# Attention and soft MoE on one core: another layout of the row-sum transfers, the norm's scaling and mask in one instruction, a new order, and eight combinations of the left half in a row

## The chip, the core and the metric

The kernel runs on one core of a Trainium2 chip. The metric is device time in microseconds (us) of one execution. TensorE (PE in the rows) does the matrix products and transposes, VectorE (DVE) and ScalarE (ACT) read and write PSUM and SBUF, GpSimd (POOL) works on SBUF, and SyncE (SP) issues nearly all transfers. Each engine runs its own instructions in the order written for it and waits on semaphores for the others.

## What is computed

Eight batches of eight heads, 576 positions, width 64. Each head has causal softmax attention and a memory read, mixed by a gate; the result goes through a soft mixture of eight experts.

```python
scores = scale * q @ k.T ; causal mask ; a = softmax(scores)          # per head
local = a @ v
q_p = phi(q)                                                          # elu + 1
mem_out = (q_p @ M_prev) / (q_p . z_prev + 1e-6)
x = g * mem_out + (1 - g) * local                                     # -> (4608, 512)
logits = x @ phi
d = softmax over all 4608 rows ; slot_input = d.T @ x                 # 8 experts x 4 slots
slot_out = relu(slot_input @ w1) @ w2
out = softmax over slots(logits) @ slot_out
```

All data is float32 (the scores are made from a high and a low part of q and k, three products each).

## The kernel before

**Pairs.** Two heads are handled together: 32 pairs, written `@0` to `@31`. `SEQ` is a list of some 2480 step names in the order in which they are issued; `name@n:slots` calls `op_name(n)` and says which PSUM bank it takes. `EV` says for movable steps whether ScalarE (`a`), GpSimd (`p`) or VectorE (`v`) does them. So `SEQ` and `EV` fix the order on every engine, the SP queue among them.

**One pair.** `loadq`, `loadk`, `loadv`, `loadm` fetch inputs. `qhi`, `qlo`, `kn`, `kl` make the high and low parts in the single buffers `X` and `K2`; they can be written only after the last score product of the pair before. `s4`, `s3`, `s2`, `s1`, `sa` (line 399, 418) are the score products of the four 128-row blocks and of the first 64 rows; `max` (line 469) masks and takes the row maximum, `exp` (line 478) the exponent and the row sum. `t`, `tf`, `ta` transpose the probabilities on TensorE (lines 565, 571, 575), `te`, `tfe`, `tae` bring them to SBUF, `av`, `ava` and `u4` (lines 603 to 629) multiply by v and the memory. `mo`, `xm`, `xa` (lines 643 to 655) scale and add into `xt`.

**The row sums' way.** Nine sums per row block stand in a 128 x 9 tile. `rec` inverts them times the gate, `rt` transposes them on TensorE to 9 x 128, `rte` copies them to `rts`, `rrw` writes them to DRAM (`rs`), and `rrr` reads them back, spread over 64 partitions for each head, into `rm` (576 wide). `mo` and `xa` need `rm`.

**The norm's way.** `norm` (line 522) makes q_p . z in PSUM; `neps` adds 1e-6 and multiplies by the gate, `nmk` multiplies by a mask, `nred` sums and inverts, `nrw` writes 4.5 KB to DRAM (`rd`), `nrr` reads it back spread into `rb`, and `qn` (line 554) multiplies q_p by it; `u4` needs `qn`.

**Weights.** `w@0` to `w@46` are loads of 512 KB each of the experts' weights, put among the steps: 29 go to buffers of their own (`w@0` to `w@28`), the others into buffers of the attention as these come free (`WORD`). All go through the SP queue, as do the small transfers above.

**Behind the pairs.** The `x` and `y` steps do the dispatch softmax and slot inputs. Then `f1` (line 949) and `f2` (line 966) are the experts' two layers, for the output's left half (`dh` 0) and right half (`dh` 1); `piece(k)` issues k parts of the right half's second layer. `comb(dh, t4)` (line 1011) makes a 512-row block of the output half, copies it by ScalarE and VectorE, and writes 512 KB out. `g1` and `g2` (lines 997, 1001) scale and sum the expert outputs ahead of the combinations. `fl` steps are matmuls without use, to keep TensorE going while it waits.

## Time and profile before

| | |
|---|---|
| median of 3 runs | 455.71 us (452.76, 455.71, 455.92) |
| profiled execution's own time | 454.65 us |
| its span, first to last instruction | 452.9 us |
| around the span | 1.75 us |
| busy: TensorE, VectorE, ScalarE, GpSimd | 424.7, 344.2, 332.8, 153.5 us |
| transferred | 97.42 MB |

A row of the timeline gives start and length of a merged group of like instructions, and in square brackets the time that the engine had been idle ahead of it and what ended that. TensorE's matmuls are pipelined, so lengths overlap. Transfers of the SP queue have issue times only; when they landed shows in whoever waited for them.

### The profile page before, as it was taken

The page shows a single profiled execution, that of the slowest core. Times are in us where ns is not written, and L with a number is a line of the kernel's source. Part 1 is how long each engine was busy: PE and PEld are TensorE (multiplying, and loading weights), DVE is VectorE, ACT ScalarE, POOL GpSimd, SP SyncE. Part 2 cuts the span into 40 slices and gives each one's busy share as a digit, 9 for nine tenths or more (in the row PEclk, how much of TensorE's full clock was granted, in tenths as well). Part 3 has the DMA queues.
Part 4 walks back from the last instruction along what each step waited for, and adds up shares of the span by engine and source line. Part 5 has one row for each costly group of instructions (what it writes and reads, how often), then busy time and mean ns, then how long its engine had stood idle before and what let it go on. Part 6 is the DMA issues. An engine that isn't in the chain of part 4 may idle for free.

```text
span 452.9 us, 12441 instructions
## 1 busy us (share of the span) xinstructions
PE 424.7 (94%) x4364; PEld 281.2 (62%) x4364; DVE 344.2 (76%) x1200; ACT 332.8 (73%) x947; POOL 153.5 (34%) x165
## 2 busy tenths in 40 slices
PE   8997999999899999999899999999999988999981
PEld 4764766666666766776566665766666655635540
DVE  5886889989799898889786996998989852431541
ACT  4997888979796988889778896989789861221431
POOL 2453443434344443353342364336343510000000
PEclk9999999999999999999999999999999999999997
DMA  4587647677856757765867558547664399999888
GB/s 157 151 253 205 190 111 241 199 204 224 236 175 199 217 152 201 221 207 153 284 194 225 162 153 237 143 143 203 178 175 127 86 335 316 334 375 397 271 289 283
DMA packets 65710, 97.42 MB, mean 215 GB/s; under 512 B 14704, under 2 KB 41072, under 8 KB 65648
## 3 DMA queue, kind: packets, MB, share of 16 engines
...
q14 instruction: 27, 0.22, 0.1%
q10 hardware_dynamic: 288, 0.09, 0.1%
...
## 4 chain that ended last, share of the span: by engine, by line
PE 64%; DVE 13%; DMA 11%; issue 4%; ACT 3%; SPq 2%; POOL 1%; DVEq 0%; POOLq 0%; ACTq 0%
PE psS L399 11%; PE psT L603 11%; PE psT L565 10%; DMA rm<-rs 6%; PE psT L624 5%; DVE P L469 4%; PE pf L966 3%; PE pf L949 3%; PE psT L727 3%; PE psT L571 2%; PE pp L1011 2%; DMA m<-in_M_dram 2%; PE psT L522 2%; DVE xt L643 2%; DMA rb<-rd 2%
## 5 line engine op out<-in xcount | busy, mean ns | idle before, releaser
L478 ACT ACTIVATE P<-P,nm 128x320 f32<-128x320 f32 (+4 forms) x288 | 166.1, 587 | 7.7 <-DVE nm L469 7.1
L469 DVE CUSTOM_DVE_ANT_0 P<-psS,mq 128x192 f32<-128x192 f32 (+3 forms) x256 | 133.6, 548 | 9.9 <-PE psS L399 8.8
L333 ACT COPY at<-psT 128x512 f32<-128x512 f32 (+1 forms) x187 | 94.3, 553 | 29.9 <-PE psT L565 11.4
L399 PE MATMUL psS<-K,X 64*128 64x288 f32 (+3 forms) x960 | 88.2, 319 | 3.6 <-DVE nm L469 3.4
L565 PE MATMUL psT<-cs,P 128*128 128x128 f32 x640 | 87.1, 276 | 4.4 <-DVE xt L654 2.4
L399 PEld LDWEIGHTS psS<-K,X 64*128 64x128 f32 x960 | 69.3, 185 | 25.9 <-issue 9.1
L603 PE MATMUL psT<-at,mq 128*64 128x256 f32 (+3 forms) x512 | 83.5, 443 | 0.0
L565 PEld LDWEIGHTS psT<-cs,P 128*128 128x128 f32 x640 | 70.8, 142 | 10.8 <-issue 4.2
L478 ACT ACTIVATION_READ_ACCUMULATOR P<-P,nm 128x1 f32 x288 | 57.2, 199 | 0.0
L385 POOL TENSOR_TENSOR X<-mq,X 128x512 fp32r<-128x512 f32 x31 | 40.8, 1315 | 24.0 <-DVE X L336 10.7
L391 POOL TENSOR_TENSOR K<-kq,K 128x576 fp32r<-128x576 f32 x27 | 38.5, 1428 | 10.0 <-DVE nm L469 5.3
L603 PEld LDWEIGHTS psT<-at,mq 128*64 128x64 f32 x512 | 28.8, 136 | 17.8 <-issue 9.3
L624 PE MATMUL psT<-kq,m 64*64 64x512 f32 x64 | 34.2, 614 | 1.3 <-DVE kq L554 1.3
L625 PE MATMUL psT<-at,mq 64*64 64x512 f32 x64 | 34.2, 615 | 0.0
L627 PE MATMUL psT<-kq,m 64*64 64x512 f32 x64 | 34.2, 615 | 0.0
L626 PE MATMUL psT<-at,mq 64*64 64x512 f32 x64 | 34.2, 614 | 0.0
L643 DVE TENSOR_TENSOR xt<-psT,rm 128x448 f32<-128x448 f32 (+7 forms) x60 | 23.8, 435 | 13.6 <-DMA rm<-rs 5.3
L338 POOL TENSOR_SCALAR X<-mq 128x512 fp32r<-128x512 f32 x21 | 13.0, 619 | 53.2 <-PE psT L489 20.9
L509 POOL TENSOR_SCALAR kq<-mq 128x576 f32<-128x576 f32 x22 | 15.4, 700 | 39.2 <-PE psT L629 39.0
L338 POOL TENSOR_SCALAR K<-kq 128x576 fp32r<-128x576 f32 x17 | 11.8, 691 | 49.3 <-PE psS L399 35.8
L516 DVE SCALAR_TENSOR_TENSOR kq<-mq,kq 128x576 f32<-128x576 f32 x32 | 26.1, 814 | 2.2 <-ACT mq L512 2.0
L336 DVE COPY at<-psT 128x512 f32<-128x512 f32 (+2 forms) x45 | 25.0, 563 | 3.2 <-PE psT L565 1.8
(198 smaller groups left out, 686.9 us busy)
## 6 DMA issues: line engine op xcount, KB each, us to landing
...
```

What stands on the lines that cost most here:

```text
L333: nc.scalar.copy(o, i)
L385: ALU_ENG[ev("qlo", n)].tensor_tensor(out=X[:, 1, :], in0=st[n]["q"][:, 64:576], in1=X[:, 0, :].bitcast(F32), op=ALU.subtract)
L391: ALU_ENG[ev("kl", n)].tensor_tensor(out=K2[:, 1, :], in0=st[n]["k"][:, 0:S], in1=K2[:, 0, :].bitcast(F32), op=ALU.subtract)
L399: nc.tensor.matmul(out(h), X[ROW[h], x, 128 * i - 128:128 * i], K2[ROW[h], y, o + k0:o + k1], start=(x, y) == (0, 0), stop=(x, y) == (0, 1))
L469: nc.vector.tensor_tensor_reduce(out=sm, in0=src, in1=msk, op0=ALU.add, op1=ALU.min, scale=-0.125, scalar=3.0e38, accum_out=s["nm"][:, J:J ...
L478: nc.scalar.activation(sm, sm, AF.Exp, scale=-1.0, bias=s["nm"][:, J:J + 1], accum_out=s["sum"][:, J:J + 1])
L565: nc.tensor.transpose(out=ps[:, 256 * x + 128 * h:256 * x + 128 * h + 128], in_=chunk(n, i, h, c), identity=ident)
L603: nc.tensor.matmul(s["oa"][ROW[h], 512 - w:512], vt[:, c, ROW[h]], at[:, base + 512 * h:base + 512 * h + w], start=first, stop=s["parts"] ...
L624: nc.tensor.matmul(om[ROW[0], :], s["m"][ROW[0], 0:64], s["qp"][ROW[0], 64:576], start=True, stop=True)
L625: nc.tensor.matmul(w2(s["oa"][ROW[1], :]), vt[ROW[0], 4, ROW[1]], af[ROW[0]], start=first, stop=s["parts"] == 5)
L626: nc.tensor.matmul(w2(s["oa"][ROW[0], :]), vt[ROW[1], 4, ROW[0]], af[ROW[1]], start=first, stop=s["parts"] == 5)
L627: nc.tensor.matmul(om[ROW[1], :], s["m"][ROW[1], 0:64], s["qp"][ROW[1], 64:576], start=True, stop=True)
```

## The change

Five edits.

**Sums' transfers.** The nine sums are put in another order (four blocks of head 0, the first rows of both, four blocks of head 1), so that `rrw` is one transfer of 9 x 128 instead of three, and `rrr` three instead of two: 64 x 512 and 64 x 64 for head 0, 64 x 576 for head 1.

**Norm.** `neps` and `nmk` become one VectorE instruction with a table `mg` made once by `gate` (mask times gate). Before, `neps` was on ScalarE in 12 pairs and on VectorE in 20, `nmk` on GpSimd in 24 and on VectorE in 8.

**A new order.** `SEQ` and `WORD` are new throughout, and `EV`: on GpSimd stand 21 `kn` (17 before), 25 `qhi` (21), 29 `kl` (27), 30 `qlo` (31), 24 `qrelu` (22); on ScalarE 10 `kn` (15), 4 `qhi` (6), 144 `te` (139), 5 `x5e` (none); on VectorE 16 `te` (21), 3 `kl` (5), 3 `qhi` (5), 8 `qrelu` (10), 2 `x5e` (7). All four conversions of a pair are on GpSimd in 18 pairs (14 before).

**Fillers.** 13 filler matmuls become 8: the four of `fl.4@0`, ahead of the second pair's scores, give way to two more groups of transposes of the first pair, and `fl.5.s` at the last pair's wait is a `fl.2.s`.

**Combinations.** Eight combinations of the left half are issued in a row, and the ninth behind `g1(1)`.

```diff
-loadq@1 qhi@0 kn@0 loadm@0 qlo@0 loadk@1 qrelu@0 kl@0 gate@0 s4@0:01 max.40@0 qexp@0 max.41@0 exp.40@0 qphi@0 fl.2@0:0
+loadk@1 qhi@0 kn@0 qrelu@0 loadq@1 qlo@0 loadm@0 kl@0 qexp@0 loadv@0 gate@0 s4@0:01 qphi@0 max.41@0 max.40@0 exp.41@0 fl.2@0:0
...
     def op_gate(n):
         nc.vector.tensor_scalar(out=rm[:, 976:1056], in0=rm[:, 976:1056], scalar1=1.0, scalar2=None, op0=ALU.add)
-        nc.vector.tensor_scalar(out=epg, in0=gc[:, :, 9], scalar1=1e-6, scalar2=None, op0=ALU.mult)
+        nc.vector.tensor_tensor(out=mg, in0=maskn.rearrange("a (o u) -> a o u", o=1).broadcast_to([128, NP, 16]),
+                                in1=gc[:, :, 9:10].broadcast_to([128, NP, 16]), op=ALU.mult)
...
     def op_rrw(n):
         rts = st[n]["rts"]
-        rd = st[n]["rs"] = drm.tile([2, S], F32, name="rs")
-        for h in range(2):
-            nc.sync.dma_start(out=rd[h, 64:S].rearrange("(i x) -> i x", i=4), in_=rts[4 * h:4 * h + 4])
-        nc.sync.dma_start(out=rd[:, 0:64].rearrange("h (j x) -> j h x", j=1), in_=rts[8:9].rearrange("j (h x) -> j h x", h=2))
+        rd = st[n]["rs"] = drm.tile([9, 128], F32, name="rs")
+        nc.sync.dma_start(out=rd, in_=rts)
 
     def op_rrr(n):
-        for h in range(2):
-            nc.sync.dma_start(out=rr[ROW[h]], in_=st[n]["rs"][h].rearrange("(o x) -> o x", o=1).broadcast_to([64, S]))
+        rd = st[n]["rs"]
+        z = rd[0:1]
+        for o, w, x, h in ((64, 512, 0, 0), (0, 576, 576, 1), (0, 64, 512, 0)):
+            nc.sync.dma_start(out=rr[ROW[h], o:o + w], in_=bass.AP(tensor=z.tensor, offset=z.offset + x, ap=[[0, 64], [1, w]]))
...
     def op_neps(n):
         rn = st[n]["rn"] = sml.tile([128, 144], F32, name="rn", bufs=1)
-        if ev("neps", n) == "a":
-            nc.scalar.activation(rn, st[n]["nps"][:, 0:144], AF.Identity, bias=epg[:, n % NP:n % NP + 1], scale=gc[:, n % NP, 9:10])
-        else:
-            nc.vector.tensor_scalar(out=rn, in0=st[n]["nps"][:, 0:144], scalar1=1e-6, scalar2=gc[:, n % NP, 9:10], op0=ALU.add, op1=ALU.mult)
-
-
-    def op_nmk(n):
-        rn = st[n]["rn"].rearrange("a (u x) -> a u x", x=9)
-        ALU_ENG[ev("nmk", n)].tensor_tensor(out=rn, in0=rn, in1=maskn.rearrange("a (u o) -> a u o", o=1).broadcast_to([128, 16, 9]), op=ALU.mult)
+        nc.vector.scalar_tensor_tensor(out=rn.rearrange("a (u x) -> a u x", x=9), in0=st[n]["nps"][:, 0:144].rearrange("a (u x) -> a u x", x=9), scalar=1e-6,
+                                       in1=mg[:, n % NP].rearrange("a (u o) -> a u o", o=1).broadcast_to([128, 16, 9]), op0=ALU.add, op1=ALU.mult)
...
     piece(1)
-    for t4 in range(NQ):
+    for t4 in range(NQ - 1):
         comb(0, t4)
     piece(13)
     g1(1)
+    comb(0, NQ - 1)
     g2(1)
     for t4 in range(NQ):
         comb(1, t4)
```

Three places where the order moves, as the instructions stand on an engine (numbers behind a name tell buffers apart).

**SP queue, pairs 0 and 1** (`rs<-rts` and `rm<-rs` are the sums' transfers, `rd<-rq` and `rb<-rd` the norm's, `w0` to `w2` the weights). Before:

```order
L504 DMA rm_105<-rs_323 64x576 x2
L544 DMA rd_394<-rq_379 128x9
L769 DMA w0_396<-in_w1_dram 128x1024
L376 DMA m_402<-in_M_dram 128x96
L371 DMA mq_102<-in_v_dram 128x640
L499 DMA rs_432<-rts_428 4x128 x2
L500 DMA rs_432<-rts_428 2x1x64
L550 DMA rb_455<-rd_394 64x4x144 x2
L769 DMA w1_474<-in_w1_dram 128x1024
L361 DMA mq_102<-in_q_dram 128x704
L366 DMA kq0_103<-in_k_dram 128x640
L504 DMA rm_105<-rs_432 64x576 x2
```

Now:

```order
L498 DMA rm_105<-rs_335 64x512
L498 DMA rm_105<-rs_335 64x576
L498 DMA rm_105<-rs_335 64x64
L355 DMA mq_102<-in_q_dram 128x704
L365 DMA mq_102<-in_v_dram 128x640
L370 DMA m_411<-in_M_dram 128x96
L492 DMA rs_421<-rts_409 9x128
L537 DMA rb_430<-rd_346 64x4x144 x2
L355 DMA mq_102<-in_q_dram 128x704
L498 DMA rm_105<-rs_421 64x512
L498 DMA rm_105<-rs_421 64x576
```

The two weight loads between the sums of pair 0 and those of pair 1 are gone from here; the first weight load now stands behind pair 3's sums, and one k load has moved behind pair 1's `rm`.

**SP queue, the last pair** (`rs_5987` before and `rs_5927` now are pair 31's sums, `rb_6010` and `rb_5936` its norm). Before:

```order
L544 DMA rd_5948<-rq_5935 128x9
L771 DMA K2_5951<-in_w2_dram 128x1024
L771 DMA P3_5956<-in_w2_dram 128x1024
L371 DMA mq_102<-in_v_dram 128x640
L499 DMA rs_5987<-rts_5978 4x128 x2
L500 DMA rs_5987<-rts_5978 2x1x64
L771 DMA mq_102<-in_w2_dram 128x1024
L550 DMA rb_6010<-rd_5948 64x4x144 x2
L771 DMA P3_6043<-in_w2_dram 128x1024
L504 DMA rm_105<-rs_5987 64x576 x2
```

Now:

```order
L531 DMA rd_5872<-rq_5862 128x9
L758 DMA P4_5878<-in_w2_dram 128x1024
L758 DMA P3_5889<-in_w2_dram 128x1024
L365 DMA mq_102<-in_v_dram 128x640
L492 DMA rs_5927<-rts_5920 9x128
L537 DMA rb_5936<-rd_5872 64x4x144 x2
L758 DMA kq0_5957<-in_w2_dram 128x1024
L498 DMA rm_105<-rs_5927 64x512
L498 DMA rm_105<-rs_5927 64x576
L498 DMA rm_105<-rs_5927 64x64
```

One weight load that stood ahead of `rb` now stands behind it, and one that stood ahead of `rm` stands behind that.

**TensorE, the last instructions** (line 1011, now 998, is `comb`; line 1001, now 988, `g2(1)`; `x36` counts matmuls). Before:

```order
L966 MATMUL pf<-w_6426,at 32x256
L966 MATMUL pf<-w_6428,at 32x256
L966 MATMUL pf<-w_6430,at 32x256
L966 MATMUL pf<-w_6432,at 32x256
L1001 MATMUL pp<-xk,cs 128x256
L1011 MATMUL pp<-xk,cT 128x256 x36
```

Now:

```order
L953 MATMUL pf<-w_6358,at 32x256
L953 MATMUL pf<-w_6360,at 32x256
L953 MATMUL pf<-w_6362,at 32x256
L953 MATMUL pf<-w_6364,at 32x256
L998 MATMUL pp<-xk,cT 128x256 x4
L988 MATMUL pp<-xk,cs 128x256
L998 MATMUL pp<-xk,cT 128x256 x36
```

The four matmuls of the left half's ninth combination stand between the last product of the second layer and `g2(1)`.

## Rows read from the trace of the kernel before

**Rows 1.** The page: busy time, share of the span and instructions, by engine.

```profile
PE 424.7 (94%) x4364; PEld 281.2 (62%) x4364; DVE 344.2 (76%) x1200; ACT 332.8 (73%) x947; POOL 153.5 (34%) x165
```

**Rows 2.** Busy time by stretch: length, each engine, clock, DMA share, GB/s.

```profile
50.00:100.00 50.00, 49.97 (x506) 35.10 (x502) 44.58 (x164) 43.06 (x122) 19.39 (x21) 1.00 0.67 197
365.00:380.00 15.00, 12.26 (x115) 7.79 (x113) 5.32 (x15) 6.46 (x20) 1.79 (x2) 1.00 1.04 327
```

**Rows 3.** Timeline of TensorE: rows with an idle time ahead of them.

```profile
14.10 1.06 PE L399 MATMUL psS<-K,X 64*128 64x288 f32 x12 [0.56 <-DVE nm L469]
...
38.95 0.71 PE L399 MATMUL psS<-K,X 64*128 64x320 f32 x6 [2.34 <-DVE nm L469]
...
110.11 0.63 PE L565 MATMUL psT<-cs,P 128*128 128x128 f32 x4 [0.15 <-DVE ext L336]
122.62 0.45 PE L522 MATMUL psT<-kq,m 128*32 128x144 f32 x8 [1.62 <-DMA m<-in_M_dram]
...
222.88 0.63 PE L565 MATMUL psT<-cs,P 128*128 128x128 f32 x4 [1.54 <-DVE xt L643]
...
358.58 0.28 PE L489 MATMUL psT<-cs,r 128*9 128x128 f32 x1 [0.35 <-DVE r L484]
...
380.50 0.61 PE L624 MATMUL psT<-kq,m 64*64 64x512 f32 x1 [1.16 <-DVE kq L554]
```

**Rows 4.** Timeline of VectorE: three waits for transfers.

```profile
38.14 0.23 DVE L654 TENSOR_TENSOR xt<-psT,rm 128x64 f32<-128x64 f32 x1 [3.27 <-DMA rm<-rs]
...
379.59 0.76 DVE L554 TENSOR_TENSOR kq<-kq,rb 128x576 f32<-128x576 f32 x1 [5.57 <-DMA rb<-rd]
382.28 0.22 DVE L654 TENSOR_TENSOR xt<-psT,rm 128x64 f32<-128x64 f32 x1 [1.93 <-DMA rm<-rs]
```

**Rows 5.** Timeline of the SP queue at the last pair: start and length of issues.

```profile
369.46 0.60 SPq L499 DMA_DIRECT2D rs<-rts  x2
370.11 0.61 SPq L500 DMA_DIRECT2D rs<-rts  x1
371.14 0.36 SPq L771 DMA_DIRECT2D mq<-in_w_dram  x1
371.61 1.39 SPq L550 DMA_DIRECT2D rb<-rd  x2
373.87 0.36 SPq L771 DMA_DIRECT2D P<-in_w_dram  x1
374.57 1.11 SPq L504 DMA_DIRECT2D rm<-rs  x2
```

**Rows 6.** Instructions by line and shape: count, busy us, mean ns, idle before.

```profile
L529 DVE TENSOR_SCALAR rn<-psT,rm 128x144 f32<-128x144 f32 x20 | 7.3, 363 | 2.4 <-PE psT L522 2.3
L527 ACT ACTIVATE rn<-psT,rm 128x144 f32<-128x144 f32 x12 | 5.7, 479 | 1.5 <-PE psT L522 1.4
L534 POOL TENSOR_TENSOR rn<-rn,rm 128x144 f32<-128x144 f32 x24 | 11.7, 489 | 33.5 <-ACT rn L527 24.8 <-DVE rn L529 8.5
L746 DVE SCALAR_TENSOR_TENSOR acc<-acc,al,psT 128x256 f32<-128x256 f32 x14 | 6.5, 467 | 0.6 <-PE psT L742 0.4 <-ACT at L333 0.2
```

**Rows 7.** The chain that ended last, in its last part: start, length, what.

```profile
427.29 5.79 PE pf L966 x104
...
433.10 0.49 DVE xk L997
...
433.64 0.71 PE pp L1001 x2
...
434.80 0.72 PE pp L1011 x8
```

**Rows 8.** Timeline of GpSimd: first and last of the four conversions of pair 15.

```profile
165.70 0.89 POOL L338 TENSOR_SCALAR K<-kq 128x576 fp32r<-128x576 f32 x1 [6.29 <-PE psS L399]
...
168.53 1.27 POOL L385 TENSOR_TENSOR X<-mq,X 128x512 fp32r<-128x512 f32 x1
```

**Rows 9.** Timeline of TensorE: the first score products of pair 15.

```profile
170.80 1.05 PE L399 MATMUL psS<-K,X 64*128 64x288 f32 x12
```

More of the change, by code (lines that the diff above doesn't have):

```diff
@@ new lines @@
+t.3@9:1 w@5 max.a@10 te.1@9 max.20@10 t.4b@9:2 w@6 tae@9 te.3@9 max.30@10 t.4a@9:3 exp.a@10 qhi@11 tf@9:0 max.21@10
+te.4a@9 max.31@10 norm@10:1 qlo@11 exp.11@10 rrr@9 av.0@9:3 max.10@10 exp.21@10 neps@10 te.4b@9 tfe@9 ava@9:1 qn@9
+loadq@12 s4@11:01 exp.20@10 nred@10 loadk@12 exp.40@10 nrw@10 av.3@9 max.41@11 av.2@9 w@7 exp.31@10 x2s@1 u4@9:0
+exp.10@10 exp.30@10 max.40@11 av.1@9 qrelu@11 loadm@11 exp.41@11 rec@10 s1@11:0 xa@9 loadv@10 exp.40@11 s3@11:1 x1d@1
+mo@9 qexp@11 s2@11 nrr@10 xm@9 t.1@10:2 kn@12 rt@10:1 max.11@11 t.3@10:3 rte@10 te.1@10 kl@12 x5@1:0 sa@11 rrw@10
@@ new lines @@
+max.10@27 te.3@26 qlo@28 rrw@26 max.30@27 t.2@26:2 tae@26 w@26 te.1@26 x5@5:0 max.31@27 tf@26:3 w@27 te.2@26 kn@28
+t.4b@26:1 max.20@27 loadq@29 exp.30@27 tfe@26 av.0@26:2 kl@28 te.4b@26 max.11@27 max.21@27 exp.20@27 rrr@26 norm@27:3
+x4.1@5:1 x5e@5 neps@27 qn@26 exp.40@27 s4@28:01 nred@27 exp.11@27 nrw@27 exp.10@27 av.3@26 max.40@28 av.1@26 loadk@29
+exp.31@27 x4a.1@5 ava@26:0 av.2@26 exp.a@27 max.41@28 exp.21@27 u4@26:3 rec@27 rt@27:1 qrelu@28 loadv@27 s1@28:0
+loadm@28 s3@28:1 qexp@28 max.11@28 mo@26 s2@28 rte@27 rrw@27 ta@27:1 xa@26 t.3@27:2 kn@29 tae@27 nrr@27 max.31@28
@@ new lines @@
+rte@30 loadm@31 qexp@31 rrw@30 s1@31:1 xa@29 exp.40@31 s2@31 nrr@30 mo@29 t.4b@30:1 max.30@31 t.4a@30:3 te.4b@30 w@29
+xm@29 t.1@30:0 te.4a@30 w@30 t.3@30:1 qphi@31 te.1@30 rrr@30 t.2@30:2 te.3@30 max.10@31 tf@30:3 max.20@31 te.2@30
+ta@30:0 norm@31:1 w@31 tae@30 exp.30@31 x4.1@6:2 neps@31 exp.10@31 nred@31 av.0@30:0 qn@30 exp.20@31 max.a@31 x4a.1@6
+nrw@31 tfe@30 x5@6:1 max.21@31 w@32 ava@30:2 exp.a@31 av.3@30 max.31@31 av.2@30 w@33 exp.21@31 max.11@31 u4@30:3
+exp.31@31 exp.11@31 av.1@30 x5e@6 rec@31 xa@30 rt@31:1 mo@30 loadv@31 t.3@31:2 rte@31 t.1@31:1 rrw@31 te.3@31 xm@30
@@ L198 @@
+yz@y y12@y y10.1@y fl.1@0:2 w@46 y12e@y y10e.1@y y10e.0@y
 """.split()
@@ L244 @@
[L244 to L247 removed]
+        qhi@0 qlo@0 kl@0 qlo@1 te.4a@0 rte@0 qn@0 qrelu@2 tae@1 te.4b@1 tfe@1 tae@2 te.4a@3 qn@3 rte@4 x2a@0
```

413 lines of the change are left out of this document (195 added, 218 removed).

## Prediction, made blind

> **What bounds the kernel now.** I read the page first. It shows TensorE busy for 424.7 of 452.9 us, so no engine but TensorE can be short of time over the whole [rows 1]. Then the busy times by stretch. In an ordinary stretch of the pairs, 50 to 100 us, TensorE is busy for 49.97 of 50 us, and VectorE and ScalarE for 44.6 and 43.1: less work on those two gives nothing there of itself [rows 2]. What a new order can win is the time that TensorE stands. So the third view was TensorE's timeline, with the idle time ahead of each row [rows 3]. There are four kinds of it.
>
> First, the fill: 0.56 us ahead of pair 1's scores and 2.34 us at 38.95 us [rows 3]. VectorE's timeline tells why the second: it stood 3.27 us for pair 1's sums (`rm`) [rows 4]. Second, between 50 and 365 us there are 12 idle times of 0.15 us or more, the first at 110.11 and the last at 358.58 us, 6.5 us in all; the two largest, 1.62 and 1.54 us, end with a late transfer, of M and (through VectorE's `mo`) of the sums [rows 3]. Third, the end of the pairs: the queue moves 327 GB/s at a full DMA share [rows 2], because weights are loaded into the freed buffers, and the last pair's two small transfers wait their turn: `rb` is issued at 371.61 and is used at 379.59 us, `rm` is issued at 374.57 and used at 382.28 [rows 4, 5]. TensorE runs fillers and still stands 1.16 us [rows 3]. Fourth, the turn between the output's halves: the last product of the second layer ends at 433.08 us, `g1` and `g2` follow, and the first combination of the right half starts at 434.80 [rows 7].
>
> **The norm's instruction.** Removed are 20 VectorE instructions of 363 ns, 12 of ScalarE of 479 ns, and the mask, of which 24 on GpSimd took 489 ns [rows 6]. Added are 32 on VectorE that no row shows. From below they cost 363 ns as the plain scaling of the same 144 columns, from above 467 ns as the same kind of instruction on 256 columns [rows 6]; I take 370, as the size decides. VectorE gets 12 more of them, some 4 us, and loses its 8 masks and several conversions; ScalarE loses 5.7 us, GpSimd 11.7 us [rows 6]. All of it lies beside TensorE's products, so the sum has nothing for it. If that cover were gone, VectorE's 12 x 0.37 = 4.4 us would be the price. The way from `norm` to `rd` gets shorter by about 0.5 us and one engine change, which only helps the last pair, and there `rb` waits behind the sums anyway.
>
> **The sums' transfers.** Three issues of 0.60 us together for two and 0.61 for the third [rows 5] become one. As the single one has the plain shape of one of the pair, I take 0.3 us; so the write starts 0.9 us earlier for its last part. `rrr` issues three times instead of two, at 1.11 us for two [rows 5] 0.55 us more, before the last part lands. The way from `rte` to `mo` is shorter by 0.35 (first rows of head 0) to 0.9 us. In most pairs it hides; it is worth something only where `rm` is late.
>
> **The fill.** In the changed order no weight load stands ahead of pair 1's sums (two did, each 512 KB; at the 327 GB/s of [rows 2] 1.6 us each, 3.2 us in all, about the 3.27 us that VectorE stood). The bounds are 0 and 2.34 us, what TensorE stood; I take 2.0. Ahead of pair 1's scores stand transposes of pair 0 in place of four fillers. Those are useful work moved into a time that was lost; bounds 0 and 1.5 (the idle 0.56 and as much again in fillers); I take 0.5, because ScalarE, which must copy the transposes out, is the next in line. The weight loads that left have to go somewhere: 29 of them now stand between pair 4 and pair 30.
>
> **The ordinary pairs.** By the listing of the order, more of TensorE's work stands between `rrr` and its use (in the median about 0.7 us more), and fewer bytes between `rte` and `rrr`. Three of the twelve idle times are of that kind, the largest of them 1.54 us [rows 3]. The two last answers of this order differ in sign: the window in which GpSimd refills `X` and `K2` gets shorter by some 0.4 us in the median pair. Bounds: 3 us gained (those three waits gone) and 3 us lost (as many new ones elsewhere); I take 1.0 gained.
>
> **The last pair.** `rb` was held at the queue by the sums' write and by one weight load: its issue came 2.15 us after the first write's [rows 5]. Now it follows one issue, so it is issued 1.7 us earlier. The queue is full, so what counts is also what lies ahead: 512 KB less for `rb` and for `rm` each, 1.6 us at 327 GB/s [rows 2]. Both bounds nearly agree. Since u4 waits for `rb` and `xa` for `rm`, both must come earlier, and both do: 1.6 us. The end of ScalarE's exponents of the last pair, which releases `rt` and so `rrw`, comes earlier by the norm's 0.48 us [rows 6], of which I take 0.2. That is 1.8 us; bounds 0.9 (the larger part eaten by something late upstream) and 3. Fewer fillers there cost nothing, as they stood in idle time.
>
> **The halves.** Of the 1.72 us from 433.08 to 434.80 us, the ninth combination fills a part: its matmuls (0.72 us for eight [rows 7]) run while `g1` (0.49 us) is on VectorE, and `g2` follows. The first row of combinations gets shorter by those 0.72 us and by what they waited there for copies (some 0.3, an estimate); `g2` waits for them 0.2 us longer than for `g1`: I take 0.8 us; bounds 0 and 1.2. The output's transfers are issued as blocks are ready, and the end of the span follows the first block of the right half, so this gain reaches the end. The left half's last block now goes out later, in a time in which the queue would stand.
>
> **Sum.** 2.0 + 0.5 + 1.0 + 1.8 + 0.8 = 6.1 us. The profiled execution took 454.65 us (span 452.9 and 1.75 around it): 448.5 us. The median of the three runs is 1.06 us above that execution, and the runs lie between 452.76 and 455.92; on the median's footing the sum is **449.6 us**, which I forecast.
>
> **Rivals.** *Nothing to measure.* The waits between 50 and 365 us come back elsewhere, and the fill's gain with them: 29 weight loads stand in a shorter stretch, so some other pair's sums, `rb` or M get the turn behind a load. For it speaks that a late transfer ended the two largest of the twelve waits [rows 3], and that every load of 512 KB holds the queue for 1.6 us wherever it stands; against it that the sums' way has become shorter. Left are the last pair and the halves: 2.6 us, so about 453, and 455 if the pairs lose 2.
>
> *Slower, through GpSimd.* All four conversions are on GpSimd in 18 pairs, 14 before. In pair 15 the first starts at 165.70 and the last ends at 169.80 us, and the scores that need them start at 170.80: 1.0 us of room [rows 8, 9]. The shorter window takes nearly half of it, and in a few pairs all. If something ahead of them in GpSimd's queue is late (its `qn` waits for `rb`), the conversions stand behind it, and TensorE's scores behind those. From 0.6 us in each of the 18 pairs on it eats the gain, and at 0.8 us each, 14 us, the time is 464. Against it: GpSimd loses 24 masks, which stood in the same queue.
>
> The Trainium skill has a rule that speaks for this rival: by the page SBUF — State Buffer, section Who interferes with whom, VectorE and GpSimd share a port pair, and a VectorE instruction with two SBUF inputs and a GpSimd instruction that reads SBUF block each other for a whole instruction, while ScalarE waits for nobody; moving conversions from ScalarE to GpSimd would then stretch both. The trace agrees so far that one such conversion took 0.89 us [rows 8]. By the rule alone the 10 conversions more, each stretched as far, would cost a few tenths of a microsecond each on GpSimd.
>
> *The transfers hidden, the rest bound elsewhere.* If the last pair's chain is held by something other than `rb` and `rm` (the weights that the second layer needs), its 1.8 us go: 451.4. The full queue [rows 2] speaks for it; that the trace names `rb` and `rm` themselves as what VectorE waited for [rows 4], against.
>
> **How the numbers follow.** The forecast has 0.50, nothing to measure 0.30, the hidden transfers 0.08, slower through GpSimd 0.12. About 1%, 4.6 us, is what a measurement of this kernel tells from no change. Faster by over 1% means below 451.1 us: the forecast (449.6) with most of its own range, 446 to 451.5, and a small part of the others, so 0.50; slower means above 460.3: 0.09 of GpSimd's 0.12; 0.41 is left for within 1%. The low end is 445.5: the forecast with the better bounds of the pairs and the last pair (3 and 3 in place of 1 and 1.8), and a little of the fill's. The high end takes in nothing to measure with its losses: 456.5. Below and above are left some 0.2.
>
> **What would show it.** Right: TensorE has no idle time over 1 us between 25 and 45 us; the last pair's `rb` is used some 8 us behind its issue still, but by 378 us if the pairs ran as before, with the first expert product 1.8 us earlier against the last pair's scores; the gap from the second layer's last product to the right half's first combination holds the ninth's matmuls; the new instruction takes 0.36 to 0.47 us. Wrong: idle times of TensorE ahead of first score products, with GpSimd's conversions named; new waits for `rb`, M or `rm` that sum to over 5 us between 50 and 365; an end that waits for the output's transfers by more than before.

## The result, and the profile after

The changed kernel takes **450.92 us** in the median (446.80 to 456.19), the kernel before 455.71 (452.76 to 456.62 with the runs made beside it). The ratio is 0.9897, interval 0.9854 to 0.9940: 1.0% faster, 4.7 us. Forecast was 449.6 us with a range of 445.5 to 456.5. (Ratios here leave out executions more than 1.5% above the fastest of their kernel; medians hold all.) The profiled execution took 450.06 us, 4.6 less than that of before; its span is 448.3 us. The line numbers of the changed kernel are 6 to 13 lower than those of before.

The page of the changed kernel, busy time by engine, beside [rows 1]:

```profile
PE 422.1 (94%) x4354; PEld 282.5 (63%) x4354; DVE 338.6 (76%) x1190; ACT 328.3 (73%) x938; POOL 151.7 (34%) x152
```

Busy time by stretch of the changed kernel, columns as in [rows 2]:

```profile
25.00:50.00 25.00, 24.90 (x248) 17.94 (x241) 21.66 (x82) 21.68 (x61) 13.21 (x13) 1.00 0.63 181
50.00:100.00 50.00, 47.65 (x491) 32.82 (x491) 41.23 (x151) 41.34 (x120) 20.37 (x21) 1.00 0.61 177
365.00:380.00 15.00, 13.19 (x138) 9.34 (x137) 5.94 (x12) 3.30 (x7) 0.00 (x0) 0.89 0.86 293
...
367.00:369.00 2.00, 1.84 (x11) 1.87 (x12) 1.30 (x3) 0.79 (x2) 0.00 (x0) 0.63 0.98 386
369.00:371.00 2.00, 2.00 (x11) 2.00 (x10) 0.00 (x0) 0.88 (x3) 0.00 (x0) 0.51 0.85 203
```

From 25 us on the fill is dense: 24.90 of 25 us, with no idle time where 2.34 us stood in [rows 3]. Ahead of that it is not: of the first 25 us TensorE is busy for 21.36, where it was 22.93. The first ordinary stretch is worse than in [rows 2]: 47.65 of 50 us, not 49.97. And from 367 to 371 us TensorE's granted clock is about half, the 1.2 GHz level. Three rows of TensorE's timeline in the changed kernel, with the idle time ahead of them, and what ran at the low clock:

```profile
66.77 0.54 PE L393 MATMUL psS<-K,X 64*128 64x288 f32 x4 [0.41 <-POOL K L331]
68.25 0.80 PE L393 MATMUL psS<-K,X 64*128 64x288 f32 x8 [0.95 <-POOL K L385]
...
367.16 1.59 PE L552 MATMUL psT<-cs,P 128*128 128x128 f32 x8 [1.81 <-DVE xt L642]
368.55 1.06 PE L558 MATMUL psT<-cs,P 128*128 128x128 f32 x4
369.40 1.06 PE L714 MATMUL psT<-cs,xt 128*128 128x128 f32 x4
370.25 1.82 PE L552 MATMUL psT<-cs,P 128*128 128x128 f32 x12
371.91 0.27 PE L562 MATMUL psT<-cs,P 128*64 128x128 f32 x1
```

VectorE at the last pair in the changed kernel, beside [rows 4]. The wait that is left is for `rm` of pair 30. In this profile the norm's product with `rb` waits for nothing, and `xa` of the last pair waits for TensorE and no longer for `rm`:

```profile
366.54 0.23 DVE L641 TENSOR_TENSOR xt<-psT,rm 128x64 f32<-128x64 f32 x1 [1.69 <-DMA rm<-rs]
...
372.86 0.76 DVE L541 TENSOR_TENSOR kq<-kq,rb 128x576 f32<-128x576 f32 x1
376.98 0.22 DVE L641 TENSOR_TENSOR xt<-psT,rm 128x64 f32<-128x64 f32 x1 [3.36 <-PE psT L616]
```

That is an exception. Here TensorE had lost 1.81 us, and more to the low clock, just ahead. In four profiles of this order without that low clock (a_y9, a_k, a_lead, a_split, see below) VectorE still waits 1.79 to 2.20 us for `rb` and 2.00 to 2.42 for the last `rm`. In a_y9:

```profile
378.86 0.76 DVE L541 TENSOR_TENSOR kq<-kq,rb 128x576 f32<-128x576 f32 x1 [2.01 <-DMA rb<-rd]
381.74 0.23 DVE L641 TENSOR_TENSOR xt<-psT,rm 128x64 f32<-128x64 f32 x1 [2.12 <-DMA rm<-rs]
```

The SP queue at the last pair, beside [rows 5]. One write in 0.29 us, three reads in 1.74 us:

```profile
365.76 0.29 SPq L492 DMA_DIRECT2D rs<-rts  x1
367.65 1.26 SPq L537 DMA_DIRECT2D rb<-rd  x2
368.96 1.18 SPq L758 DMA_DIRECT2D kq<-in_w_dram  x1
...
372.00 1.74 SPq L498 DMA_DIRECT2D rm<-rs  x3
```

The new norm instruction, beside [rows 6], 302 ns each:

```profile
L520 DVE SCALAR_TENSOR_TENSOR rn<-psT,rm 128x144 f32<-128x144 f32 x32 | 9.7, 302 | 7.4 <-PE psT L516 6.8
```

The chain of the changed kernel at the turn between the halves, beside [rows 7]. The second layer ends at 428.29 us, the ninth combination follows, and the right half's first starts at 430.06:

```profile
424.84 3.45 PE pf L953 x64
428.29 0.64 PE pp L998 x8
428.94 0.68 PE pp L988 x2
...
430.06 0.72 PE pp L998 x8
```

**One execution is not enough here.** All profiles below were cut at the same five places of TensorE's and VectorE's timelines: the first score product of pair 4 and of pair 31, the maximum of `y4`, the first product of the first layer, the last of the second. "Idle" is the sum of TensorE's idle times over 0.3 us between pair 4's and pair 31's scores. "Low" counts stretches of granted clock 0.5 ahead of the last product. All in us.

| profile | start to pair 4 | pair 4 to 31 | idle in it | pair 31 to `y4` | `y4` to first layer | both layers | span | low |
|---|---|---|---|---|---|---|---|---|
| before | 45.16 | 310.07 | 4.70 | 29.65 | 7.77 | 40.38 | 452.9 | 0 |
| b_fill | 44.10 | 315.33 | 7.57 | 28.62 | 7.77 | 40.38 | 456.1 | 2 |
| b_sums | 45.88 | 313.32 | 6.76 | 28.29 | 7.77 | 40.39 | 455.6 | 2 |
| b_norm | 43.88 | 310.77 | 3.67 | 28.53 | 7.77 | 40.38 | 451.4 | 1 |
| b_comb | 43.43 | 312.28 | 5.64 | 29.49 | 7.77 | 39.79 | 452.9 | 1 |
| after | 42.69 | 308.79 | 7.89 | 28.27 | 8.75 | 39.79 | 448.3 | 1 |
| a_rm30 | 42.93 | 310.78 | 9.14 | 30.12 | 8.76 | 39.78 | 452.4 | 1 |
| a_hot | 42.80 | 312.50 | 9.97 | 27.75 | 8.76 | 39.79 | 451.5 | 0 |
| a_y9 | 42.61 | 314.91 | 10.18 | 26.68 | 8.60 | 39.78 | 452.6 | 2 |
| a_k | 42.90 | 313.39 | 9.45 | 26.54 | 8.75 | 39.79 | 451.2 | 1 |
| a_lead | 42.55 | 313.30 | 9.05 | 26.38 | 8.75 | 39.79 | 450.7 | 2 |
| a_split | 42.67 | 312.85 | 9.58 | 26.35 | 8.76 | 39.79 | 451.0 | 1 |
| a_best | 42.65 | 310.11 | 8.01 | 26.50 | 8.61 | 39.78 | 447.6 | 0 |

Names with b_ are the kernel before with one edit, with a_ the changed kernel with one. The stretches from `y4` on repeat to 0.02 us; those in the pairs differ from one execution to the next by some microseconds, with the late transfers and the low clock. So the pairs are compared over several profiles.

### The profile page after: what moved, and what is told of

It is laid out like the page before. It is cut to its first block, busy times and chain, and to the rows that moved or that the text cites. A ratio compares the mean times of both kernels' runs of the same rounds, so it can differ in the third digit from the quotient of the medians.

```text
span 448.3 us, 12344 instructions
## 1 busy us (share of the span) xinstructions
PE 422.1 (94%) x4354; PEld 282.5 (63%) x4354; DVE 338.6 (76%) x1190; ACT 328.3 (73%) x938; POOL 151.7 (34%) x152
## 4 chain that ended last, share of the span: by engine, by line
PE 68%; DMA 14%; DVE 8%; ACT 3%; issue 2%; SPq 2%; POOL 1%; DVEq 0%; ACTq 0%; POOLq 0%
PE psS L393 14%; PE psT L590 12%; PE psT L552 12%; PE psT L611 5%; DMA rm<-rs 5%; DMA rb<-rd 3%; PE pf L953 3%; PE pf L936 3%; DVE P L463 3%; PE psT L714 3%; PE psT L558 2%; DMA kq<-in_k_dram 2%; PE pp L998 2%; DMA rs<-rts 2%; PE psT L516 2%
## 5 line engine op out<-in xcount | busy, mean ns | idle before, releaser
L472 ACT ACTIVATE P<-P,nm 128x576 f32<-128x576 f32 (+4 forms) x288 | 166.0, 585 | 6.6 <-DVE nm L463 5.9
L463 DVE CUSTOM_DVE_ANT_0 P<-psS,mq 128x448 f32<-128x448 f32 (+3 forms) x256 | 133.1, 548 | 17.1 <-PE psS L393 16.6
L326 ACT COPY at<-psT 128x512 f32<-128x512 f32 (+1 forms) x194 | 97.0, 550 | 26.7 <-PE psT L552 14.9
L590 PE MATMUL psT<-at,mq 128*64 128x128 f32 (+3 forms) x512 | 84.0, 443 | 0.0
L385 POOL TENSOR_TENSOR K<-kq,K 128x576 fp32r<-128x576 f32 x29 | 41.2, 1420 | 20.3 <-ACT K L326 19.2
L379 POOL TENSOR_TENSOR X<-mq,X 128x512 fp32r<-128x512 f32 x30 | 39.4, 1315 | 14.0 <-ACT xk L326 5.5
L503 POOL TENSOR_SCALAR kq<-mq 128x576 f32<-128x576 f32 x24 | 16.8, 701 | 56.8 <-PE psT L616 54.1
L331 POOL TENSOR_SCALAR X<-mq 128x512 fp32r<-128x512 f32 x25 | 16.1, 642 | 52.6 <-PE psS L393 35.1
L331 POOL TENSOR_SCALAR K<-kq 128x576 fp32r<-128x576 f32 x21 | 14.9, 707 | 54.9 <-PE psS L393 42.4
L541 POOL TENSOR_TENSOR kq<-kq,rb 128x576 f32<-128x576 f32 x16 | 23.1, 1446 | 12.6 <-DMA rb<-rd 9.9
```

The source lines that it names most:

```text
L326: nc.scalar.copy(o, i)
L379: ALU_ENG[ev("qlo", n)].tensor_tensor(out=X[:, 1, :], in0=st[n]["q"][:, 64:576], in1=X[:, 0, :].bitcast(F32), op=ALU.subtract)
L385: ALU_ENG[ev("kl", n)].tensor_tensor(out=K2[:, 1, :], in0=st[n]["k"][:, 0:S], in1=K2[:, 0, :].bitcast(F32), op=ALU.subtract)
L463: nc.vector.tensor_tensor_reduce(out=sm, in0=src, in1=msk, op0=ALU.add, op1=ALU.min, scale=-0.125, scalar=3.0e38, accum_out=s["nm"][:, J:J ...
L472: nc.scalar.activation(sm, sm, AF.Exp, scale=-1.0, bias=s["nm"][:, J:J + 1], accum_out=s["sum"][:, J:J + 1])
L590: nc.tensor.matmul(s["oa"][ROW[h], 512 - w:512], vt[:, c, ROW[h]], at[:, base + 512 * h:base + 512 * h + w], start=first, stop=s["parts"] ...
```

## The experiments

**First question: which part brings what?** Four runs make one part of the change in the kernel before.

*b_fill*: the two weight loads that stood ahead of pair 1's sums go behind the sums of pairs 3 and 4.

```diff
-nrw@1 w@0 max.41@2 ... xm@0 w@1 te.3@1 ... rrr@3 ... rrr@4
+nrw@1 max.41@2 ... xm@0 te.3@1 ... rrr@3 w@0 ... rrr@4 w@1
```

> The kernel before with one thing moved: its first two weight loads (512 KB each) are issued behind the reads of pair 3's and pair 4's sums and no longer ahead of pair 1's. My theory: these two loads alone made VectorE stand 3.27 us for pair 1's sums and TensorE 2.34 us at 38.95 us, so that idle time falls under 0.5 us, pair 4's scores start some 2 us earlier than before, and the end comes 1.5 to 2.3 us earlier: about 453 against the median of 455.7. Rival one: the sums are late for another reason (their three writes, the reads' own time), the idle time stays above 1.5 us, and the time is that of before. Rival two: the idle time goes but comes back as a late transfer in pairs 4 to 6, where the two loads now stand: pair 8's scores start less than 0.7 us earlier than before, and the time is within 0.7 us of before.

Measured: ratio 1.0018 (0.9968 to 1.0067). At the fill, the SP queue's timeline of b_fill:

```profile
29.35 0.55 SPq L361 DMA_DIRECT2D mq<-in_q_dram  x1
29.95 0.42 SPq L366 DMA_DIRECT2D kq<-in_k_dram  x1
30.55 1.12 SPq L504 DMA_DIRECT2D rm<-rs  x2
```

And VectorE's, at the use of these sums:

```profile
37.08 0.23 DVE L654 TENSOR_TENSOR xt<-psT,rm 128x64 f32<-128x64 f32 x1 [1.97 <-DMA rm<-rs]
```

VectorE still waits 1.97 us for pair 1's sums, with no weight load ahead of them; q and k, 672 KB, are issued just ahead. And the moved loads show again: TensorE stands 2.14 us up to 60.88 us for pair 4's `rm`. So rival two holds for the time. How much of the fill's wait the loads made is not shown: with them ahead of these sums VectorE waited 3.27 us in the profile before, 3.71 in b_sums, 2.22 in b_comb and not at all in b_norm, and 1.97 without them lies within that.

*b_sums*: the sums' transfers alone (one write, three reads, the columns' order with them).

```diff
-        for h in range(2):
-            nc.sync.dma_start(out=rd[h, 64:S].rearrange("(i x) -> i x", i=4), in_=rts[4 * h:4 * h + 4])
-        nc.sync.dma_start(out=rd[:, 0:64].rearrange("h (j x) -> j h x", j=1), in_=rts[8:9].rearrange("j (h x) -> j h x", h=2))
+        nc.sync.dma_start(out=rd, in_=rts)
```

> The kernel before with the sums' transfers alone changed (one write in place of three, three reads in place of two), in the order of before. My theory: the sums' way is some 0.35 to 0.9 us shorter, which shows where VectorE waited for rm: 0.3 to 0.9 us less of the 2.34 us at 38.95 us, and in the last pair the read of the norm is issued some 1.7 us earlier than at 371.61 against the write, so that VectorE waits for rb 1 to 1.7 us less than 5.57 us and u4 starts up to 1.6 us earlier against the last pair's scores. Together 1 to 2.5 us: 453 to 454.7. Rival: the third read and the smaller packets take back what the single write gives, rb and rm land as late as before behind the weight loads, and the time is within 0.5 us of before.

Measured: ratio 1.0006 (0.9960 to 1.0052): the rival. In the last pair the read of the norm is issued 0.81 us behind the write's issue (373.42 and 374.23 us), where 2.15 us lay in [rows 5]; yet VectorE waits 5.42 us for `rb`, against 5.57 in [rows 4], since `rb` is used 7.8 us after its issue as before (8.0). The earlier issue was worth nothing here, with the queue full.

*b_norm*: the norm's instruction alone.

```diff
-            nc.vector.tensor_scalar(out=rn, in0=st[n]["nps"][:, 0:144], scalar1=1e-6, scalar2=gc[:, n % NP, 9:10], op0=ALU.add, op1=ALU.mult)
+        nc.vector.scalar_tensor_tensor(out=rn..., in0=st[n]["nps"]..., scalar=1e-6, in1=mg[:, n % NP]..., op0=ALU.add, op1=ALU.mult)
```

> The kernel before with the norm's scaling and mask in one VectorE instruction, the order otherwise as before (the mask's step is dropped). My theory: the instruction takes 0.30 us as in the changed kernel, all of it beside TensorE's products; the way from the norm's product to its write is some 0.5 us shorter, hidden in all pairs but the last; the time is within 0.7 us of before. Rival: VectorE is in places the engine that others wait for (TensorE waited for its nm, r and xt), and 12 instructions more on it make idle times of TensorE ahead of scores: 1 us or more slower.

Measured: ratio 0.9983 (0.9938 to 1.0029), 302 ns an instruction. It lies beside other work, as expected.

*b_comb*: the ninth combination of the left half behind `g1`.

```diff
-    for t4 in range(NQ):
+    for t4 in range(NQ - 1):
         comb(0, t4)
     piece(13)
     g1(1)
+    comb(0, NQ - 1)
```

> The kernel before with the ninth combination of the left half behind the gate of the right half, all else as before. My theory: the last product of the second layer ends 0.6 to 1.0 us earlier against the first layer's start, the right half's first combination follows it by some 1.6 to 1.8 us, and the end comes 0.6 to 0.8 us earlier: about 455 against 455.7. Rival: the output's transfers set the end (their queue runs without a gap in the last 15 us), and the time is that of before within 0.2 us although the right half's first combination starts earlier.

Measured: ratio 0.9986 (0.9951 to 1.0022); in the trace both layers take 39.79 us in place of 40.38, and the right half's first combination follows the second layer's end by 1.77 us, as in the changed kernel (1.72 before). So 0.59 us, repeated to 0.01 us in the changed kernel's profiles; the times alone could not have shown it. From the second layer's end to the last instruction it takes 19.8 to 20.1 us in the four profiles without this edit and 19.9 to 20.5 in the nine with it, so most of the gain reaches the end.

None of the four parts alone gives what a time can show. By exclusion most of the gain lies in the new order. That is argued and not shown: the new order with the old transfers and the old norm was not run, nor were the parts together.

**Second question: what took back a part of the gain?** Four runs change one thing in the changed kernel.

*a_rm30*: two weight loads go behind the reads of pair 30's sums, for which TensorE stood 1.81 us.

```diff
-te.4b@30 w@29 xm@29 t.1@30:0 te.4a@30 w@30 t.3@30:1 te.1@30 rrr@30
+te.4b@30 xm@29 t.1@30:0 te.4a@30 t.3@30:1 te.1@30 rrr@30 w@29 w@30
```

> The changed kernel with its weight loads 29 and 30 issued behind the reads of pair 30's sums, not ahead of them. In the changed kernel VectorE waits 1.69 us for these sums at 366.54 us, TensorE stands 1.81 us up to 367.16, and from 367 to 371 us its granted clock is 0.5 to 0.6 (the 1.2 GHz level), which stretches eight transposes to 1.59 us and four to 1.06. My theory: the wait goes, TensorE does not stand, its clock stays at 1.00 from 365 to 380 us, and the end comes 2 to 3.3 us earlier (1.5 to 1.8 of the wait, up to 1.6 of the clock), about 448. Rival one: the sums are late for their own write and reads, the wait shrinks by less than 0.5 us, and the time is within 0.7 us of the changed kernel. Rival two: the wait goes, but the last pair's own transfers, or the weights of the first layer, are late by as much, and the first layer starts less than 1 us earlier.

Measured: ratio 0.9963 (0.9927 to 0.9999), above the changed kernel's 0.9897, though the intervals meet. The wait for `rm` is gone, but the last pair's v now stands behind those loads. TensorE's timeline of a_rm30:

```profile
375.35 1.98 PE L590 MATMUL psT<-at,mq 128*64 128x512 f32 x4 [3.48 <-DMA mq<-in_v_dram]
```

Rival two: a transfer of the last pair's own, its v.

*a_hot*: seven products that nobody reads, in the stand of 1.81 us.

```diff
-rt@31:1 mo@30
+rt@31:1 fl.7.s@0:0 mo@30
```

> The changed kernel with seven more products that nobody reads (256 columns each, about 0.24 us) on TensorE behind the last pair's transposed sums, in the 1.81 us in which it stands for pair 30's sums. The wait itself stays. My theory: the lower clock from 367 to 371 us is what follows that stand, so with the products in it the clock stays at 1.00, the eight transposes behind it take about 0.9 us in place of 1.59 and the four 0.45 to 0.6 in place of 1.06, and the first layer starts 1 to 2 us earlier against the moment the wait ends: a time 1 to 2 us below the changed kernel. Rival one: the clock falls at that place whatever TensorE does there: the same row of 0.5 to 0.6, the same time within 0.5 us. Rival two: the clock stays up, but the work behind it waits for other things (the copies on ScalarE and VectorE, the last transfers), and the time is within 0.5 us.

Measured: ratio 0.9899 (0.9860 to 0.9938), as the changed kernel. The clock stays at 1.00 there, but so it does at that stand in four other profiles of the changed order (a_y9, a_k, a_lead, a_split). TensorE's timeline of a_y9 at the same work:

```profile
372.77 1.06 PE L552 MATMUL psT<-cs,P 128*128 128x128 f32 x8 [1.38 <-DVE xt L642]
373.67 0.60 PE L558 MATMUL psT<-cs,P 128*128 128x128 f32 x4
374.13 0.66 PE L714 MATMUL psT<-cs,xt 128*128 128x128 f32 x4
374.62 1.50 PE L552 MATMUL psT<-cs,P 128*128 128x128 f32 x12
375.96 0.29 PE L562 MATMUL psT<-cs,P 128*64 128x128 f32 x1
```

From the first to the last of these rows it is 3.19 us here and 4.75 in the changed kernel's profile: a low stretch costs 1.6 us. The fillers did what they were meant to do, but in most executions there was nothing to prevent, and seven, 3.19 us in all where the expectation counted some 0.24 each, are about 1 us more than the stand needed (27.75 to `y4` against some 26.5). So the experiment does not settle that a stand causes the low clock; the count at the end bears on it.

*a_y9*: the accumulation of the left half goes behind the last product of y9.

```diff
-y8@y y9a.0@y y8n@y y9.3@y y8a@y y8e@y y9.2@y
+y8@y y8n@y y9.3@y y8a@y y8e@y y9.2@y y9a.0@y
```

> The changed kernel with the accumulation of the left half of the last slots (y9a.0) issued behind the last product of y9 in place of between its two halves, as it stood in the kernel before. In the changed kernel TensorE stands 0.37 us up to 385.15 for it. My theory: that idle time goes and the first layer starts 0.3 to 0.6 us earlier against the maximum of y4 (8.75 us in the changed kernel, 7.77 before); the rest of the difference is work that the new order moved from ahead of y4 to behind it. Rival: TensorE does not wait for the accumulation but for the transfer of the maxima beside it (y8, ngm, ag, es), and the 8.75 us stay within 0.15.

Measured: the stand of 0.37 us goes, but only 0.15 us of 8.75 are won: the moved accumulation itself ends next. In a_y9 it ends at 390.78 us and `y10` starts at 390.83, while the transfer of the maxima (`y8` to `es`) had ended at 390.02. So neither the theory's 0.3 us nor the rival's reason. Ratio 0.9909 (0.9864 to 0.9953).

*a_k*: weight loads 0 and 8 go behind k of pairs 6 and 13.

```diff
-xm@3 ta@4:2 w@0 t.4a@4:3 ... loadk@6 ... kl@6
+xm@3 ta@4:2 t.4a@4:3 ... loadk@6 ... kl@6 w@0
```

> The changed kernel with two of its weight loads moved: load 0 from ahead of pair 6's k to behind that pair's conversions, load 8 from ahead of pair 13's k to behind that pair's conversions. In the changed kernel GpSimd waits 2.68 us for k of pair 6, and TensorE stands 0.41 and 0.95 us at 66.77 and 68.25; at 143.49 it stands 0.98 us behind ScalarE, which waited 1.48 us for k. My theory: 512 KB at the queue's pace of some 300 GB/s are 1.7 us, so each k comes that much earlier; the idle times of pair 6 go by 0.8 to 1.36 us, that at 143.49 by 0.5 to 0.98, and the time falls by 1.3 to 2.3 us. Rival: the loads are late for the transfers ahead of them other than the weights (v, q, rb), the waits shrink by less than 0.4 us together; or they go and the moved loads make the next pair's transfers late, and the time is within 0.5 us.

Measured: ratio 0.9857 (0.9799 to 0.9914) from four runs. The stands at 66.77 and 68.25 us are gone and that at 143.49 is down to 0.51; pair 8's scores start 2.5 us earlier than in the kernel before, 0.2 in the changed kernel's profile. But the idle time from pair 4 to 31 is 9.45 us as in the other profiles, and the engines' waits for k from 45 to 350 us sum to 18.0 us, against 10.5 in the changed kernel's profile: others came. Theory and rival hold in part, and the interval does not part this kernel from the changed one.

**Third question: what makes the pairs' transfers late?** The changed order stands 9.0 us from pair 4 to 31 in the mean of the five profiles that leave the pairs untouched (after, a_rm30, a_hot, a_y9, a_best), the order of before 5.7.

*a_lead*: for 20 pairs k is issued earlier. *a_now*: the first 29 weight loads are issued behind the pairs.

```diff
 # a_lead, pair 6 as an example
-u4@3:0 max.11@4 ... max.40@5 loadk@6 qexp@5
+loadk@6 u4@3:0 max.11@4 ... max.40@5 qexp@5
 # a_now
-... w@0 ... w@28 ... mo@31 w@40
+... mo@31 w@40 w@0 ... w@28
```

> The changed kernel with nothing but the issue of k moved: for the 20 pairs whose k is issued later than 7.5 us of TensorE's work ahead of its conversion, it is issued earlier, by 0.4 to 4.1 us. In the profiles so far TensorE stands (idle times over 0.3 us) 7.9 to 10.2 us between pair 4's and pair 31's scores in the changed order, and 3.7 to 7.6 us in the order of before; waits of the conversions for k are in every profile of the changed order. My theory: the changed order issues k too late (in the median 6.3 us of TensorE's work ahead in place of 7.7), so with k earlier the waits for k fall under 2 us together, TensorE's idle time in these pairs falls to 5 to 7 us, and the time is 2 to 4 us below the changed kernel: 447 to 449. Rival one: the queue is full there for the weight loads, whatever is issued first, so an earlier k makes v, M, rb or rm late instead: idle 8 us or more, time within 1 us. Rival two: the waits move into the last pair or the fill.

> The changed kernel with its first 29 weight loads, 15 MB in all, issued behind the pairs and no longer between pairs 4 and 30. The first layer then waits for them, so only the pairs are to be read. Theory one (the weight loads fill the queue and make the other transfers late): TensorE's idle time from pair 4's to pair 31's scores falls from 7.9 to 10.2 us to 3 us or less. Theory two (the order issues k and q too late of itself): the idle time stays at 6 us or more, and the conversions still wait for k. If both carry, it ends between 3 and 6.

Measured: a_lead 0.9834 (0.9785 to 0.9883), idle 9.05 us; the median of its ten executions is 451.17 us, as the changed kernel's 450.92. a_now, one execution, 474.77 us in all, idle 2.66 us and pair 4 to 31 in 303.44. The next four fences are the engines' waits for transfers from 45 to 350 us, by line: sum, count and longest. The kernel before:

```profile
DVE xt L643 <- DMA rm<-rs: 3.9, 3, 1.6
POOL kq L554 <- DMA rb<-rd: 3.4, 1, 3.4
```

The changed kernel:

```profile
POOL K L331 <- DMA kq<-in_k_dram: 7.3, 4, 2.7
...
POOL kq L541 <- DMA rb<-rd: 4.8, 3, 3.0
POOL X L331 <- DMA mq<-in_q_dram: 4.3, 1, 4.3
ACT K L326 <- DMA kq<-in_k_dram: 3.2, 3, 1.5
```

The run a_lead:

```profile
POOL kq L541 <- DMA rb<-rd: 8.8, 3, 4.0
DVE xt L641 <- DMA rm<-rs: 6.9, 3, 3.5
...
DVE xt L630 <- DMA rm<-rs: 3.0, 1, 3.0
...
POOL K L331 <- DMA kq<-in_k_dram: 2.6, 1, 2.6
```

And a_now, without weight loads in the pairs:

```profile
POOL kq L541 <- DMA rb<-rd: 5.8, 4, 3.2
POOL K L331 <- DMA kq<-in_k_dram: 3.0, 2, 2.5
ACT K L326 <- DMA kq<-in_k_dram: 1.5, 1, 1.5
```

With k earlier, the waits for k fall from 10.5 to 5.0 us in all and not under 2; those for `rm` rise from 3.0 to 9.9 and for `rb` from 7.0 to 8.8: rival one. Without the loads k and `rb` are still waited for, 4.5 and 5.8 us, but TensorE hardly stands for it: theory one. All waits for transfers in this stretch sum to 11.2 us there and to 29 to 47 in the five profiles with the changed pairs. So, by one execution without them, the weight loads make some 6 to 7 us of the idle time. Which transfer pays differs between executions: the profile before has no wait for k, the four other profiles of its order 8.4 to 10.2 us. That the order sets how much is paid is likely, as the order of before stands 5.7 us; but it has 26 loads in this stretch, not 29, so the two are not parted. The loads are the largest saving in sight, but they must be read at some time.

*a_split*: each of the 29 loads in two halves, the second later.

```diff
-        nc.sync.dma_start(out=t, in_=w1[4 * i[0] + g, i[1], i[2]])
+        nc.sync.dma_start(out=t[:, 0], in_=w1[4 * i[0] + g, i[1], i[2]][:, 0])   # 4 us later: [:, 1]
```

> The changed kernel with each of its first 29 weight loads issued as two of 256 KB, the second 4 us of TensorE's work behind the first; nothing else moves, and the bytes are the same. Without these loads in the pairs TensorE stood 2.7 us between pair 4's and pair 31's scores, with them 7.9 to 10.2. My theory: what makes the small transfers late is that one load holds the queue 1.6 us at a stretch, so half the length takes away about half of the 6.6 us that the loads cost: idle 5 to 7 us, and no single stand over 1.3 us, so that the lower clock after such stands is gone from the pairs too; time 447 to 449. Rival: it is the queue's total load (share 0.6 to 0.7 over the pairs) that makes them late, however it is cut: idle 8 to 10 us, stands of 1.4 to 2 us as before, time within 1 us of the changed kernel. Rival two: rows half as long take longer to move, and idle rises above 10 us.

Measured: ratio 0.9951 (0.9901 to 1.0001), median 452.89 us, idle 9.58 us, one stand of 2.12 us with a low clock behind it. The rival: the amount counts, not the length of one load.

*a_best*: weight loads 29 and 30 behind the last pair's sums, and the edit of a_y9.

```diff
-te.4b@30 w@29 xm@29 t.1@30:0 te.4a@30 w@30 t.3@30:1 ... rrr@31 tae@31
+te.4b@30 xm@29 t.1@30:0 te.4a@30 t.3@30:1 ... rrr@31 w@29 w@30 tae@31
```

> The changed kernel with two edits, meant to beat it. Its weight loads 29 and 30 are issued behind the reads of the last pair's sums, where the queue is not full (DMA share 0.47 to 0.86 from 371 to 377 us in the changed kernel), not ahead of pair 30's sums, and not ahead of the last pair's v, which they made 3.5 us late in the run that put them just behind pair 30's sums. And the accumulation of the left half of the last slots is issued behind the last product of y9. My theory: VectorE no longer waits for pair 30's sums, the stand of 1.0 to 1.8 us that every profile of the changed order shows about 17 us behind the last pair's scores goes, and with it the lower clock that followed one in some executions; from the last pair's scores to y4 it takes 25.0 to 25.5 us (26.4 to 26.7 in the profiles of the changed order without the lower clock there, 28.3 with it), y4 to the first layer 8.6, first layer to the second's end 39.8 as before; the time is 1.3 to 2 us below the changed kernel, about 449. Rival one: pair 30's sums are late for other loads, the stand stays above 0.8 us, and only the 0.15 us of y9 are gained. Rival two: the loads now make the weights of the first layer or the output late, and the 39.8 us or the 18 us behind them grow by as much.

Measured: 449.22 us in the median (447.76 to 454.12), ratio 0.9856 (0.9800 to 0.9912). It is the kernel with the lowest median of those run, 1.7 us below the changed one, but the intervals overlap. The time is the expected one, the way to it is not: the wait for pair 30's `rm` is gone (it lay some 15 us behind the last pair's scores, not 17), yet from pair 31's scores to `y4` it takes 26.50 us and not 25.0 to 25.5, as TensorE waits for v of the last pair in its place. TensorE's timeline of a_best:

```profile
372.42 1.08 PE L590 MATMUL psT<-at,mq 128*64 128x512 f32 x4 [1.49 <-DMA mq<-in_v_dram]
```

## Why the prediction was right, and where its terms were not

The time and the range held: 450.92 us against 449.6. The sum of 6.1 us did not hold in each term. In the two profiled executions it is 4.6 us; over the table, with 1.6 us taken off for each low stretch in its column, it is 3.5.

- **The fill: 2.5 forecast, 1.5 measured.** To pair 4's scores the order of before takes 44.19 us in the mean of four profiles (before, b_sums, b_norm, b_comb), the changed order 42.73 in eight. The stand of 2.34 us is gone in all eight, but it was read from one execution: at this place the order of before stood 2.77 us in b_sums, 1.30 in b_comb and 0.18 in b_norm, 1.65 in the mean of the four and not 2.0. That the two weight loads made it is not shown (see b_fill). The step that failed is that useful work would fill the time lost ahead of pair 1's scores, worth 0.5: TensorE stands there longer, 1.07 to 1.08 us in every profile of the changed order for 0.56, and 0.6 and 0.49 us ahead of that, where the order of before did not stand. In the profile after:

```profile
9.33 1.66 PE L393 MATMUL psS<-K,X 64*128 64x448 f32 x18 [0.63 <-DVE nm L463]
11.49 0.43 PE L412 MATMUL psS<-kq,mq 128*128 128x64 f32 x2 [0.49 <-DVE nm L463]
14.84 1.25 PE L393 MATMUL psS<-K,X 64*128 64x288 f32 x12 [1.07 <-DVE nm L463]
```

So from the first score product to pair 4 the idle times of 0.15 us or more sum to 2.05 to 3.69 us in the four profiles of the order of before and still to 2.17 to 2.46 in the eight; three fillers fewer, some 0.47 us each, are most of the rest.
- **The ordinary pairs: 1.0 forecast, nothing measured.** 310.75 us in the mean of the five profiles in the order of before, 310.78 in the five that leave the changed pairs as they are. Without the 1.6 us for each low stretch the means are 312.35 and 311.42, and profiles of one order lie up to 6 us apart, so 1.0 is not excluded. The mechanism was another: fewer waits for `rm` were to save idle time, but idle time rose by 3.4 us, with k, M and v among what is late. TensorE's time at work and in small gaps fell by as much, which the prediction did not name (the small gaps alone from about 2.0 to 0.6 us; why the same products take some 2 us less besides is not settled). The first rival's mechanism, weight loads in a shorter stretch that make another transfer late, did occur; 29 of them lie between 45 and 350 us, 26 before. Its cost was about as large as that fall, not larger.
- **The last pair: 1.8 forecast, 1.4 measured.** To `y4` it takes 28.92 us in the order of before and 26.53 in the changed one (after, a_y9, a_k, a_lead, a_split): 2.4 less. But from `y4` to the first layer it takes 0.98 more, which the prediction did not cost: four transposes of x3 moved from ahead of `y4` to behind it (some 0.5 us), the stand of 0.37 us, and y10 in two parts. Up to `y4` TensorE's idle times of 0.15 us or more sum to 2.20 to 3.59 us in the order of before and to 1.35 to 1.81 in these five, and there are two fillers fewer, some 1.0 us. VectorE waits less for `rb`, 1.79 to 2.20 us or not at all in place of 4.40 to 5.61, but about as long as before for the last `rm`, except in the profile after. The step that failed is the 1.7 us by which `rb` would be issued earlier: its issue follows the write's by 1.23 to 1.91 us in these five profiles, 2.15 in [rows 5], so by 0.2 to 0.9 us. What came in its place is a shorter way: it is used 5.2 to 5.5 us behind its issue, where the prediction kept some 8. And the two did not alone set the end. TensorE's stand for pair 30's sums was not counted, and it stayed (1.81 in the profile after). In the trace of before:

```profile
370.92 0.63 PE L565 MATMUL psT<-cs,P 128*128 128x128 f32 x4 [1.82 <-DVE xt L654]
```

- **The halves: 0.8 forecast, 0.59 measured**, in every profile. The ninth's matmuls fill the time of `g1`; the estimate of 0.3 us for copies was too much.
- **The norm's instruction** took 302 ns, below the lower bound of 363. A plain scaling of the same columns was no lower bound for an instruction of another kind. It changed nothing that a time could show, as it is hidden.
- **GpSimd's chain** formed at one place, pair 6: in the five profiles that leave the changed pairs as they are, its conversions are named there ahead of idle times of 0.54 to 1.75 us of TensorE's, in the profile after at 66.77 and 68.25 us, where k was 2.68 us late ahead of them. Its price was off too: 0.34 us in each of 18 pairs eats the 6.1 us, not 0.6. The trace agrees with the rule cited from the Trainium skill (SBUF — State Buffer, Who interferes with whom). Most `kn` took 0.67 us there and most `qhi` 0.62, before and after. Those that began while VectorE's `kq<-mq,kq`, which has two inputs in SBUF, was running took longer: [rows 8] shows one of two before; in the changed kernel two of 21 `kn` took 0.82 and 1.26 us, two of 25 `qhi` 0.72 and 1.13. Where GpSimd began first, VectorE's instruction took up to 1.92 us in place of 0.75. In the profile after:

```profile
301.57 0.75 DVE L510 SCALAR_TENSOR_TENSOR kq<-mq,kq 128x576 f32<-128x576 f32 x1
301.59 1.26 POOL L331 TENSOR_SCALAR K<-kq 128x576 fp32r<-128x576 f32 x1
```

None of TensorE's idle times over 0.3 us lies within 10 us behind these four, so this cost nothing that shows.

All four terms were too large by the table, by 2.6 us together. That the forecast time still came out near has a part of luck in it: the measured gain of 4.7 us has an interval from 2.7 to 6.7.
